# A recurrent memory transformer beside a feed-forward block: half of one weight piece is loaded into the score buffers over the step boundary

## The chip, the cores and the metric

The kernel runs on one core of a Trainium2 chip. The metric is the device time in microseconds, the median of several executions. The engines are TensorE (PE; its weight loads are listed as PEld), VectorE (DVE), ScalarE (ACT), GpSimd (POOL) and SyncE (SP); SP issues most of the transfers, which 16 DMA engines carry out.

## The reference

Two blocks on the same input of 2048 tokens by 1024 values are mixed by a gate. Block A goes through the tokens in 64 segments of 32; each segment is joined by 8 memory rows, which are the output of the segment before:

```
mem = mem0
for s in range(64):
    h = concatenate([mem, x[32*s : 32*s + 32]])           # 40 rows x 1024
    q, k, v = h @ Wq, h @ Wk, h @ Wv                      # 32 heads of 128
    p = softmax(masked(q k^T * 128**-0.5))                # per head, 40 x 40
    o = (p v) @ Wo                                        # 40 x 1024
    mem, out[s] = o[:8], o[8:]
b = (gelu(x @ w_gate) * (x @ w_up)) @ w_down
g = sigmoid((x * gate_w).sum(-1))
result = g * a + (1 - g) * b
```

All inputs are bfloat16. Each of Wq, Wk, Wv and Wo is 8 MB. Segment s needs the memory that segment s-1 gave, so the 64 steps of block A run one after the other; each uses all 32 MB of weights.

## The kernel before, in words

**Pieces and slots.** Each of the four matrices is cut into 16 pieces of 128 partitions x 2048 values (512 KB): (m, u, i) is matrix m, half u of the heads, rows i of eight. Not all 64 pieces fit on the chip. `PAIRS` (line 295) names for each matrix the i whose two pieces (u = 0 and u = 1) share one slot: three of k, three of q, four of v, four of o. These 14 slots are loaded anew in each step; all other pieces stay.

**The order.** `ORDER` (line 301) and `walk` give 64 positions per step: k0, q0, v0, k1, q1, o0, v1, o1, eight pieces each. The first round of a matrix begins with its paired pieces, the second ends with them, and `at_step` swaps u in odd steps, so the piece that a slot holds at the end of a step is the one that the next step begins with. Each slot is therefore loaded once a step: `proj` (line 653) issues a piece's products on PE and calls `spent` (358), which calls `fetch` (344), and SP issues the DMA of the slot's other piece as soon as the first has been read (line 351 in the trace, tile name sl). The first k piece of a step is (k, u, 1).

**A step.** hT holds 32 columns: 24 tokens of the segment and 8 memory rows. For each eight positions PE accumulates 128x512 products in a PSUM bank (line 662), ACT copies the bank to tok (`evac`, 568), PE transposes tok and DVE copies the result into kT or qT (`trans`, 575). The other eight rows of k, q and v of the segment (the "rest") do not depend on the memory. They are made in advance, for four segments at once, by `fill` (683) from hR; `fill_evac` (697) copies a fill's bank to a staging tile, `fill_put` (706) transposes it, copies it again and POOL stores it to qk_scr (line 719), while v goes straight to v_scr in four POOL stores (line 702). Later `load_qk` (440) and `load_v` (445) bring a segment's share back into qkr and vB, and POOL's `put_rest` (722) copies qkr into kT and qT. `scores` (594) multiplies, and DVE and ACT make the softmax in buffers laid over kT (pA, pB) and qT (tA, tB, E8). `attend` (625) multiplies with vA and vB; ACT and DVE copy into oT, POOL copies columns of oT into oRc (646). After o1 (line 674, bank XO) ACT copies the bank to a_bf, PE transposes it (840), and DVE copies the memory columns into hT (843): with that copy a step ends. POOL stores a_bf to a_scr (835).

**Staging.** a_bf lies over oT. `stage` (287) lets kT, qT, oT or tok hold a fill's copy. kT, qT and oT are 1,280 bytes per partition each and lie one behind the other.

**Fills by step.** `two` (line 735) is true in steps with s%4 of 3 or 0: there a q fill (8 pieces) and a k fill are made; in the others a v fill. Called two-fill and one-fill steps below. A k fill runs around positions q1,5 to q1,7; of the other fill three pieces run before v1 in two-fill steps, three (or five) before `attend` at o1,0, and the rest behind it. Its copies to kT and qT and its store come at o1,1 and o1,5. The last steps (from 59 on) have no fills.

**Queues.** Each engine works through its instructions in program order, with waits on semaphores that the program derives from overlapping bytes. On SP, at o1,0, stand: the load of hT for the next step, the load of qkr, the load of vB (which waits for `attend`), the store of oRc; then the fetches of the next step. A named lane orders the DMAs on it: each waits for the one before. In step 0 all rest products of segments 0 to 3 (and some of 4 to 7) are made between the normal ones (`fill0`, 764).

After the steps, at about 1776 us, memory rows of the output are made from o_scr, and block B runs in about 700 us.

## Time and profile before

| What | Value |
|---|---|
| Device time, median of 3 runs | 2480.26 us (2474.82 to 2481.07) |
| The profiled execution | 2477.56 us |
| Its span, first to last instruction | 2475.7 us |
| Granted TensorE clock, mean | 0.966 |
| PE busy | 2112.3 us, 85% |
| DVE, ACT, POOL busy | 886.7, 599.6, 449.3 us |
| Bytes moved | 642.77 MB, mean 260 GB/s |
| From the first to the last copy into hT (62 steps) | 150.6 to 1775.9 us |

A row of an instruction group gives line, engine, operation, tiles (out<-in), shapes, count, busy time, mean ns and the idle time of its engine before it with what ended that. A window row gives its length, each engine's busy time with the number of instructions, the granted clock, the DMA engines' mean busy share and GB/s. A timeline row gives start, duration, engine, line and tiles, and in brackets the idle time before it. A busy PE is not PE at its peak: products on four column groups run side by side.

### The profile page before, as it was taken

How to read it: one execution, taken by the hardware profiler on the slowest of the kernel's cores; microseconds unless marked ns; L12 is line 12 of the kernel's file. 1: busy time of each engine (PE TensorE's matmuls, PEld its weight loads, DVE VectorE, ACT ScalarE, POOL GpSimd, SP SyncE). 2: the span in 40 equal slices, each digit the busy share in tenths (PEclk: the TensorE clock that was granted, in tenths of full speed). 3: DMA queues.
4: the chain of work that ended last, by engine and by line, in shares of the span. 5: the costliest groups of instructions: out<-in, count | busy, mean ns of one | idle time of the engine just before them, and what ended most of it. 6: DMA issues, size and time to landing. Idle time of an engine off the chain costs nothing.

```text
span 2475.7 us, 76524 instructions
## 1 busy us (share of the span) xinstructions
PE 2112.3 (85%) x34822; PEld 1056.5 (43%) x34822; DVE 886.7 (36%) x2090; ACT 599.6 (24%) x1204; POOL 449.3 (18%) x886
## 2 busy tenths in 40 slices
PE   2488888888888888888888888888779999999998
PEld 1144444444444444444444444444444444444443
DVE  3223333333333333333333333333304435263452
ACT  1122222222222222222222322222203213032130
POOL 5222222222222222222222222222100000000000
PEclk9799999999999999999999999999989999999999
DMA  9869888888789888888888888988894260703406
GB/s 360 320 217 321 287 301 320 292 309 319 277 316 322 279 319 313 293 324 294 311 301 292 316 315 292 318 310 290 320 299 147 77 212 1 260 29 122 167 1 221
DMA packets 280195, 642.77 MB, mean 260 GB/s; under 512 B 30344, under 2 KB 75912, under 8 KB 279872
## 3 DMA queue, kind: packets, MB, share of 16 engines
q1 hardware_dynamic: 254560, 600.74, 67.8%
q0 software_dynamic: 14944, 22.27, 3.6%
q10 hardware_dynamic: 10368, 14.88, 1.7%
q8 instruction: 273, 4.47, 0.7%
q14 instruction: 50, 0.41, 0.0%
HBM read 606.29 MB, written 31.39 MB: 258 GB/s over the span
## 4 chain that ended last, share of the span: by engine, by line
PE 50%; DMA 35%; DVE 7%; issue 3%; ACT 3%; POOL 1%; SPq 0%; ACTq 0%; POOLq 0%; DVEq 0%
DMA sl<-in_A_Wq_dram 14%; DMA sl<-in_A_Wo_dram 14%; PE pb L662 13%; PE pb L900 13%; PE pb L674 7%; PE pb L937 6%; PE pb L691 3%; PE pb L859 2%; DMA wd<-in_B_w_down_dram 2%; PE pb L578 2%; DMA sl<-in_A_Wk_dram 2%; ACT a_bf L561 1%; DMA xr_scr<-xr 1%; PE pb L840 1%; POOL gp L428 1%
## 5 line engine op out<-in xcount | busy, mean ns | idle before, releaser
L662 PE MATMUL pb<-sl,hT 128*32 128x512 bf16 x12288 | 810.7, 394 | 95.5 <-DMA sl<-in_A_Wq_dram 39.1
L662 PEld LDWEIGHTS pb<-sl,hT 128*32 128x32 bf16 x12288 | 327.5, 99 | 422.9 <-DMA sl<-in_A_Wq_dram 58.0
L674 PE MATMUL pb<-sl,oT 128*32 128x256 bf16 x8192 | 292.8, 282 | 49.8 <-DMA sl<-in_A_Wo_dram 36.4
L561 ACT ACTIVATE tok<-pb 128x512 bf16<-128x512 f32 x320 | 191.1, 597 | 535.2 <-PE pb L662 460.5
L674 PEld LDWEIGHTS pb<-sl,oT 128*32 128x32 bf16 x8192 | 205.9, 99 | 121.0 <-DMA sl<-in_A_Wo_dram 57.2
L691 PE MATMUL pb<-sl,hR 128*32 128x512 bf16 x3072 | 218.8, 391 | 8.1 <-DMA hR<-xr_scr 4.5
L900 PE MATMUL pb<-xT,wg 128*128 128x512 bf16 x896 | 211.8, 379 | 8.4 <-DVE GT L916 8.4
L900 PE MATMUL pb<-xT,wu 128*128 128x512 bf16 x896 | 211.7, 379 | 0.0
L937 PE MATMUL pb<-wd,GT 128*128 128x512 bf16 x896 | 196.2, 379 | 6.3 <-DMA wd<-in_B_w_down_dram 6.3
L646 POOL COPY oRc<-oT 128x128 bf16<-128x128 bf16 x128 | 96.9, 757 | 478.0 <-DVE oT L564 478.0
L564 DVE COPY kT<-pb 128x512 bf16<-128x512 bf16 x128 | 54.4, 425 | 289.2 <-PE pb L578 287.0
L564 DVE COPY qT<-pb 128x512 bf16<-128x512 bf16 x128 | 54.4, 425 | 276.8 <-PE pb L578 271.7
L908 ACT ACTIVATE s<-pb 128x512 f32<-128x512 f32 x112 | 66.8, 596 | 321.7 <-PE pb L900 302.2
L900 PEld LDWEIGHTS pb<-xT,wg 128*128 128x128 bf16 x896 | 86.9, 98 | 116.4 <-DVE GT L916 12.8
L937 PEld LDWEIGHTS pb<-wd,GT 128*128 128x128 bf16 x896 | 86.5, 98 | 115.3 <-DMA wd<-in_B_w_down_dram 13.2
L900 PEld LDWEIGHTS pb<-xT,wu 128*128 128x128 bf16 x896 | 87.7, 98 | 105.7
L909 DVE SCALAR_TENSOR_TENSOR tp<-s,pb 128x512 f32<-128x512 f32 x112 | 76.9, 687 | 133.7 <-ACT s L908 133.6
L607 DVE TENSOR_REDUCE st<-pb 128x8 f32<-128x320 f32 x128 | 62.9, 492 | 164.7 <-PE pb L602 164.7
L609 ACT ACTIVATE E<-pb 128x320 bf16<-128x320 f32 x128 | 56.0, 437 | 252.8 <-DVE pb L608 252.6
L606 POOL MEMSET pB<- 128x144 f32 x128 | 27.7, 216 | 491.2 <-ACT vA L561 246.5
L561 ACT ACTIVATE vA<-pb 128x512 bf16<-128x512 f32 x128 | 76.4, 597 | 155.4 <-PE pb L662 128.0
L578 PE MATMUL pb<-ident,tok 128*128 128x128 bf16 x1024 | 103.6, 225 | 11.3 <-ACT tok L561 10.2
(81 smaller groups left out, 1775.8 us busy)
## 6 DMA issues: line engine op xcount, KB each, us to landing
sl<-in_A_Wv_dram SPq DMA_DIRECT2D x268, 512.0 KB, 11.0
sl<-in_A_Wo_dram SPq DMA_DIRECT2D x268, 512.0 KB, 7.3
sl<-in_A_Wk_dram SPq DMA_DIRECT2D x205, 512.0 KB, 5.8
sl<-in_A_Wq_dram SPq DMA_DIRECT2D x205, 512.0 KB, 8.9
wd<-in_B_w_down_dram SPq DMA_DIRECT2D x56, 1024.0 KB, 6.4
wg<-in_B_w_gate_dram SPq DMA_DIRECT2D x3, 1792.0 KB, 15.6
wu<-in_B_w_up_dram SPq DMA_DIRECT2D x3, 1792.0 KB, 13.5
qkr<-qk_scr POOLq DMA_DIRECT2D x65, 64.0 KB, 6.2
```

The source lines that it names most:

```text
L561: op("act", lambda e: e.activation(o, i, ACTF.Copy), rd=rd, wr=wr)
L564: op("dve", lambda e: e.tensor_copy(o, i), rd=rd, wr=wr)
L578: ins = e.transpose(PBV[TT][:, j * 128:(j + 1) * 128], tok[:, j * 128:(j + 1) * 128], ident[:, :])
L607: op("dve", lambda e: e.tensor_reduce(nm, sS, AX.X, ALU.max, negate=True), rd=[BK(SS)], wr=[st8.r(0, 8)])
L646: op("pool", lambda e: e.tensor_copy(oRc[:, :, 16 * u:16 * u + 16].rearrange("p c x -> p x c"), oT[:, :, :, 32:40].rearrange("p g j c -> p ...
L662: ins = e.matmul(PB[bk][32 * g:32 * g + 32, :], lhsT=h[:, i, :], rhs=w[:, g * 512:(g + 1) * 512], start=(p % 8 == 0), stop=(p % 8 == 7))
L674: ins = e.matmul(PB[XO][32 * g:32 * g + 32, 0:256], lhsT=oT[:, gp_, 2 * jj + hh, 0:32], rhs=w[:, c:c + 256], start=(r == 0 and p % 8 == 0 ...
L691: ins = e.matmul(PB[b][32 * g:32 * g + 32, :], lhsT=h[:, k[2], :], rhs=w[:, g * 512:(g + 1) * 512], start=(n == 0), stop=(n == 7))
L900: ins = e.matmul(PB[bk][:, 0:FB], lhsT=w[:, kc, cc:cc + 128], rhs=xT[:, :, :, kc, :].rearrange("p t i c -> p (t i) c"), start=(kc == 0), s ...
L908: op("act", lambda e, hg=hg: e.activation(s1[:, :], hg, ACTF.Square, scale=SQ), rd=[BK(bg)], wr=[s1.r()])
L909: op("dve", lambda e, hg=hg, t=t: e.scalar_tensor_tensor(out=t[:, :], in0=s1[:, :], scalar=1.0, in1=hg, op0=ALU.add, op1=ALU.mult), rd=[BK ...
L937: ins = e.matmul(PB[bank[2 * k + hf]][:, :], lhsT=GT[:, j, tb * 128:(tb + 1) * 128], rhs=w[:, jj, hf * 512:(hf + 1) * 512], start=(j == 0) ...
```

## The change

wP is a new tile of 128 x 1024 over kT and the first 768 bytes of qT. Over the step boundary, once `attend` of the second half has read tA and tB, SP loads into wP the first half (256 KB) of the next step's first k piece (`fetch_park`), and, behind the other loads of the boundary, the first half of that slot's other piece into the slot itself (`fetch_hi`). Behind the use of the first k piece `fetch` loads only the second half of the other piece. The products of the first position read wP and the second half of the slot. So the slot's two pieces cause three transfers of 256 KB a step instead of one of 512 KB, two of them at the boundary.

To leave kT and qT free there, fills no longer stage in them: tok is the staging tile of k and q fills, oT's place that of v fills, and a_bf moves to the tail of qT. Two-fill steps now make k and v, one-fill steps q. The v fill runs four pieces before `attend`, two at o1,6 and two behind the step's last product, while ACT copies a_bf; its copy and its four stores follow the boundary, and the two PSUM banks of the projections change places for the next step. The q fill runs wholly before `attend`; its transposes follow at o1,1. The transposes of the k fill come right behind the scores, ahead of the softmax. `put_rest` of kT moves from the third to the fourth position, `put_rest` of qT and the load of the second qkr from the third to the sixteenth. On SP, qkr's load now stands behind `fetch_park`. In step 0 all k and q rest products stage in tok, and one more v fill takes the place of one q fill. memT and hR1 move to other bytes.

```diff
-        a_bf = al("a_bf", [128, 256], at=oT.off)
-        stage = {n: al(n + "S", [128, 512], at=t.off) for n, t in (("k", kT), ("q", qT), ("o", oT))}
+        a_bf = al("a_bf", [128, 256], at=qT.off + 768)
+        wP = al("wP", [128, 1024], at=kT.off)
+        stage = {"o": al("oS", [128, 512], at=oT.off), "t": tok}
...
+        IP = PAIRS["k"][0]
+        NP_ = home["k", 0, IP]
+        def src_h(k, hf):
+            m, u, i = k
+            W = {"q": A_Wq, "k": A_Wk, "v": A_Wv}[m]
+            return W[i * 128:(i + 1) * 128, 16 * u + 8 * hf:16 * u + 8 * hf + 8, :].rearrange("d h e -> d (h e)")
+        def fetch_hi(k):
+            t = slots[NP_]
+            op("sp", lambda e: e.dma_start(t[:, 0:1024], src_h(k, 0)), wr=[t.r(0, 1024)], lane="hi")
+        def fetch_park(k):
+            op("sp", lambda e: e.dma_start(wP[:, :], src_h(k, 0)), wr=[wP.r()], lane="wP")
+        def tile(k, g, parked):
+            if parked and home[k] == NP_ and g < 2:
+                return wP[:, g * 512:(g + 1) * 512]
+            return slots[home[k]][:, g * 512:(g + 1) * 512]
...
         def fetch(n):
             k, t = uses[n][done[n]], slots[n]
+            if n == NP_:
+                op("sp", lambda e: e.dma_start(t[:, 1024:2048], src_h(k, 1)), wr=[t.r(1024, 2048)], lane=f"sl{n}")
+                return
...
         def scores():
...
+        def softmax():
             op("pool", lambda e: e.memset(pB[:, :].bitcast(FP32), 0.0), wr=[pB.r()])
...
-            f1 = fill("q" if two else "v", ub, X) if G < NG else []
-            f2 = fill("k", ub, Y) if two and G < NG else []
+            fk = fill("k", ub, Y) if two else []
+            fv = fill("v", ub, X) if two else []
+            fq = fill("q", ub, X) if one else []
...
-            def start_step():
-                if s > 0:
-                    rest(0)
-                    load_qk(s, 1)
...
-                    on("k", 0, 0, lambda: fill0("k", 0, B1, "o", 1, hR1))
-                on("q", 0, 0, lambda: fill0("q", 0, B1, "q"))
+                    on("k", 0, 0, lambda: fill0("k", 0, B1, "t", 1, hR1))
+                on("q", 0, 0, lambda: fill0("q", 0, B1, "t"))
...
+                on("v", 0, 0, lambda: fill0("v", 0, B2, "o"))
                 if NG > 1:
-                    on("q", 0, 0, lambda: fill0("q", 0, B2, "o", 1, hR1))
+                    on("v", 0, 0, lambda: fill0("v", 0, B0, "t", 1, hR1))
+            else:
+                on("k", 0, 3, lambda: put_rest(kT, 1))
+                on("q", 0, 7, lambda: (put_rest(qT, 0), load_qk(s, 1)))
...
             on("v", 1, 0, lambda: scores())
+            if two:
+                on("v", 1, 0, lambda: fill_put("k", ub, G, "t", "t", "act"))
+            on("v", 1, 0, softmax)
+            on("v", 1, 0, some(fq, 5))
             on("o", 1, 0, lambda: load_h(s + 1) if not last else None)
             on("o", 1, 0, lambda: evac(bko["v", 1], vA, "act"))
+            on("o", 1, 0, some(fq, 3))
+            if one:
+                on("o", 1, 0, lambda: fill_evac("q", ub, G, bx, "t"))
+            on("o", 1, 0, some(fv, 4))
             on("o", 1, 0, lambda: attend(ub))
+            if one:
+                on("o", 1, 1, lambda: fill_put("q", ub, G, "t", "t", "dve"))
...
+            def ahead():
+                fetch_park(at_step(0, s + 1))
+                load_qk(s + 1, 0, "sp")
+                load_v(s + 1, eng="sp")
+                o_store()
+                fetch_hi(("k", 1 - (s + 1) % 2, IP))
...
+                on("o", 1, 0, ahead)
+            on("o", 1, 6, some(fv, 2))
             for p in range(64):
                 run(at.get(p, []))
                 proj(p, s)
             act_copy(a_bf[:, :], PB[XO][:, 0:256], [BK(XO)], [a_bf.r()])
+            run(fv)
...
+            if two:
+                fill_evac("v", ub, G, bx, "o")
+                X, Y = Y, X
```

## The prediction

> **What bounds the kernel now.** I read the page first (shares, the chain that ended last, the DMA issues), then the start of every step (the copy into hT at L843), then one step in windows, then the instructions around a step boundary.
>
> ```profile
> DMA  9869888888789888888888888988894260703406
> PE 50%; DMA 35%; DVE 7%; issue 3%; ACT 3%; POOL 1%; SPq 0%; ACTq 0%; POOLq 0%; DVEq 0%
> DMA sl<-in_A_Wq_dram 14%; DMA sl<-in_A_Wo_dram 14%; PE pb L662 13%; PE pb L900 13%; PE pb L674 7%; PE pb L937 6%; PE pb L691 3%; PE pb L859 2%; DMA wd<-in_B_w_down_dram 2%; PE pb L578 2%; DMA sl<-in_A_Wk_dram 2%; ACT a_bf L561 1%; DMA xr_scr<-xr 1%; PE pb L840 1%; POOL gp L428 1%
> ...
> sl<-in_A_Wv_dram SPq DMA_DIRECT2D x268, 512.0 KB, 11.0
> sl<-in_A_Wo_dram SPq DMA_DIRECT2D x268, 512.0 KB, 7.3
> sl<-in_A_Wk_dram SPq DMA_DIRECT2D x205, 512.0 KB, 5.8
> sl<-in_A_Wq_dram SPq DMA_DIRECT2D x205, 512.0 KB, 8.9
> ```
>
> DMA is 80 to 90% busy through the whole recurrent stage, the chain spends 30% of the span on weight pieces, and a 512 KB piece takes 5.8 to 11 us to land: they queue behind each other. The copy into hT closes a step:
>
> ```profile
> L843 DVE COPY hT<-pb x63: 190/192/192, 150.6 to 1775.9; 128x64 bf16<-128x64 bf16 x63
> ```
>
> 62 steps in 1625.3 us, 26.21 us each. Step 34 (1017.97 to 1043.40) in windows; behind PE, PEld, DVE, ACT and POOL stand the granted clock, the DMA share and GB/s:
>
> ```profile
> 1018.00:1020.00 2.00, 1.99 (x40) 1.01 (x44) 0.00 (x0) 0.03 (x1) 1.05 (x2) 1.00 0.47 70
> 1020.00:1022.00 2.00, 2.00 (x40) 0.93 (x36) 0.42 (x1) 0.57 (x1) 1.17 (x3) 1.00 0.89 279
> 1022.00:1026.00 4.00, 4.00 (x101) 1.93 (x93) 1.42 (x3) 1.21 (x3) 0.21 (x1) 1.00 1.04 356
> ...
> 1038.00:1040.00 2.00, 1.97 (x76) 1.56 (x76) 0.56 (x2) 1.10 (x3) 0.77 (x1) 1.00 1.04 375
> 1040.00:1042.00 2.00, 0.87 (x32) 0.31 (x22) 0.00 (x0) 0.00 (x0) 1.92 (x4) 1.00 0.72 214
> 1042.00:1044.00 2.00, 1.23 (x18) 0.51 (x22) 0.19 (x1) 0.38 (x1) 1.16 (x3) 0.85 0.22 46
> ```
>
> DMA is full from about 2 us into the step until 22 us and nearly empty around the boundary. The end of that step, in the timeline:
>
> ```profile
> 1040.64 0.40 PE L674 MATMUL pb<-sl,oT 128*32 128x256 bf16 x8 [0.19 <-DMA sl<-in_A_Wo_dram]
> 1041.98 0.40 PE L674 MATMUL pb<-sl,oT 128*32 128x256 bf16 x8 [0.94 <-DMA sl<-in_A_Wo_dram]
> 1042.43 0.38 ACT L561 ACTIVATE a_bf<-pb 128x256 bf16<-128x256 f32 x1 [2.64 <-PE pb L674]
> 1042.87 0.29 PE L840 MATMUL pb<-ident,a_bf 128*128 128x128 bf16 x2 [0.49 <-ACT a_bf L561]
> 1043.20 0.19 DVE L843 COPY hT<-pb 128x64 bf16<-128x64 bf16 x1 [4.19 <-PE pb L840]
> 1043.44 1.05 PE L662 MATMUL pb<-sl,hT 128*32 128x512 bf16 x8 [0.28 <-DVE hT L843]
> 1044.11 0.33 SPq L351 DMA_DIRECT2D sl<-in_A_Wk_dram  x1
> ```
>
> The last two Wo pieces arrive one by one; 0.5 us after the last one a_bf is copied, 1.0 us later the step ends, and 0.5 to 0.7 us into the next step its first fetch goes out. From the trace's issue and landing times, averaged over 62 steps and counted from the step's start, the pieces land at: Wk 4.9, 6.8, 8.7; Wq 10.6, 12.0, 13.5; Wv 14.9, 16.2, 17.5, 18.8; Wo 20.3, 21.7, 23.2, 24.6; then hT 24.9, qkr 25.2, vB 25.5, o_scr 25.7. The last Wo is issued near 16, so it stands in a queue that never runs dry. In one-fill steps (s%4 is 1 or 2) a_bf follows Wo by 0.5 us in almost every step; in two-fill steps on average by 0.8. So the loop is: first fetch, 14 pieces in line, last Wo, boundary. Between 1.5 us before the boundary and 1.2 us after it 2.0 to 2.3 us of DMA time (all 16 engines) lie unused.
>
> **The change, part by part.**
>
> *Half a piece leaves the full stretch.* Of the first k piece only 256 KB are fetched behind its use; 13.5 pieces stand before the last Wo. Price of half a piece: successive Wv pieces (4,096-byte rows) land 1.31 us apart, so half is 0.65; with 2,048-byte rows (Wo, 1.43 apart) the remaining half costs 0.72, the saving then is 0.60. Upper end: successive Wk pieces land 1.9 us apart, half is 0.95 to 1.0. I take 0.65, because the Wk distance holds other work (qkr, a_scr) that stays. 63 steps (1 to 63): 41 us, ends 38 and 63.
>
> *The two halves at the boundary.* Both copies go out on SP behind attend (end at 20.5 in one-fill, 21.6 in two-fill steps), so behind Wo in line: hT, issued at 19.4 to 20.8, lands 0.25 us after Wo. The parked half then lands 0.25 + 0.72 = 0.97 us after Wo; its first reader starts 1.5 us after Wo. Cover 0.5 us, cost 0. Without cover (a 128 KB store from POOL in between, 0.46 us of packet time) up to 0.3 a step, 19 us. The other half follows qkr, vB and o_scr: about 2.4 us after Wo, 0.9 into the next step, when the first new fetch barely starts. Both take 1.45 us of the 2.0 to 2.3 unused. Cost 0; traffic grows by 0.26 MB a step.
>
> *SP's order.* qkr no longer goes out before attend ends: issued some 1.5 us later and 0.7 further back, it lands at about the boundary. Its user, the POOL copy into kT, moves to the fourth piece (0.65 us in). vB is used after 10 us. Cost 0.
>
> *POOL.* The qT copy and the second qkr load move from the third to the sixteenth piece. The qT copy now waits for the store of a_bf, which lies in qT's tail: issued near -0.5, landing 4 to 5 us later, so near 4; DVE's write of qT comes at 5.0. qkr then is issued near 4.5 and lands 6.1 later (its row today), before 11; its reader is the fortieth piece, past 12. In exchange vA no longer waits for that store (21.0 us in 9 steps today, mostly covered). Cost 0; a late store costs at most 0.5 in some steps.
>
> *v fill over the boundary, in 31 steps.* Four v_scr issues of 0.556 us stand behind a_scr: POOL is free near 2.5, the kT copy ends at 2.9, DVE needs it at 3.3. Their 128 KB fall into the full stretch; today the q store (128 KB) goes out around the boundary. 4,096-byte packets on that queue take 229 ns, 32 of them on 16 engines 0.46 us; today's q store already delays the first Wk by 0.2 (5.0 against 4.8). I take 0.2 more, 6 us, ends 0 and 14. The vA copy (6.2) has to wait for these stores to read oS: last issue near 2, landing by 4.5 to 7; the Exp behind it is due at 7.9, so nothing.
>
> *Products.* Two v pieces (0.43 us) run while ACT copies a_bf, in a PE gap of 0.49. In two-fill steps the q transposes (0.33) leave the stretch after attend; the k copy on ACT comes before Exp (0.6 us against DVE's 1.0). In one-fill steps three fills (0.65) move ahead of attend, into a wait for tB of 0.85 to 0.95, and transposes (0.33) come behind it. All this frees PE where Wo binds: gain 0, ends -10 and 0. The one-fill q store goes out nearer the Wo tail than today's v stores: 0.1 in 32 steps, 3 us, ends 0 and 10.
>
> *Clock.* In one-fill steps PE waits 0.3 to 0.6 longer for Wo. The windows show half clock for 3.41 us at a time, in most cases, 30 times from step 1 to 63, after stretches of equal length with only 0.9 to 2.6 us of idle; the 52 first products of a step then take 4.63 us instead of 2.99, and the step's mean is 0.4 to 0.6 longer. Eight more such steps: 4 us, ends 0 and 10. The Trainium skill (TensorE: Matmul & The Clock Gate, Part 1) has the clock fall after a window of about 3.4 us that is idle; by that rule this term would be 0. The rows above show falls after far less idle, so the trace does not agree.
>
> *Step 0.* Its k and q results are now staged in tok alone. Today the q_k stores land 5.6, 6.4, 6.8 and 5.5 us after issue and each waits for the one before; now the copy out of PSUM, the transposes and the second copy (1.8 us) join that wait, one store leaves it and a second set of v stores enters. Following the chain I get the first attend near 119.5 instead of 115.9, and 2 us more at the last fill: 6 us, ends 0 and 12.
>
> Sum: -41 + 6 + 3 + 4 + 6 = -22. The profiled execution took 2477.56 us (span 2475.7), 2.7 below the median of the three runs, 2480.26, and inside their spread. 2477.6 - 22 = 2456.
>
> **Rivals.**
>
> *A. Another limit takes over in two-fill steps.* There a_bf follows Wo by 0.8 on average, so in part of them PE, not Wo, ends the step. If only the 32 one-fill steps gain, and the v fill costs half: -21 + 16 = -5, 2472. Against it: attend could end at 20.6 in two-fill steps (softmax behind the earliest scores at 15.9), and 2.2 us of products behind it end before the new Wo landing (24).
>
> *B. The half pieces are slow; slower than before.* They read 2,048 bytes out of every 8,192; no transfer today does that (Wo's rows are contiguous). Wo's own packets take 88 ns in the stream, but 207 at its start. A half has 8 packets on each of 16 engines. With c for its time in the full stretch the steps gain 63 x (1.31 - c) against the 19 us of small costs: nothing is left at c = 1.01 us (126 ns a packet), 0.3% is lost from 1.13 (141 ns), and at 1.66 (207 ns) the parked half also lands 0.4 us too late: 22 + 26 + 19 = 67, 2545. For it: nothing measured. Against: whole pieces, 4,096 of 8,192, run at 162 ns, the full rate. The Trainium skill (DMA: Bandwidth & Descriptors, Latency and other measured facts) reports rates falling to half for row pitches of large powers of two, from 512 KiB up; whether 8 KiB suffers no run here shows.
>
> *C. The half piece is worth what Wk's distance says*, 0.95, with the small costs at half: -60 + 9, 2427.
>
> *D. The unused time at the boundary cannot be used,* so 0.26 MB more is 0.7 us more a step: 2520. That would be the change not doing what it says. Against it: hT, qkr, vB and o_scr already run there at 0.2 to 0.3 us apiece.
>
> **Chances.** Forecast (2442 to 2466) 0.52; A 0.17; C 0.13; B 0.14; D 0.04. A measurement can tell about 0.3%, 7.4 us: faster is below 2472.8. Faster: 0.52 + 0.13 + half of A = 0.74; same: the rest of A and the mild end of B, 0.11; slower: 0.15. The range 2428 to 2488 leaves out some 0.06 below and 0.13 above.
>
> **What the new profile would show.** Right: steps of about 25.6 us; last Wo landing near 24.0 with a_bf 0.5 behind; DMA share up by about 3 points, the boundary windows near 0.7; hardly any PE wait for the parked tile at the first piece; step 0 ending near 157. Wrong: PE waiting for wP at each boundary, half-piece packets well over 100 ns (B); a_bf more than 0.8 behind Wo with unchanged steps (A); the first Wk landing later than 5 us (D); ACT waiting for tok's stores at the ninth piece.

## The result, and the profile after

The changed kernel takes 2488.49 us (median of 15 runs, 2476.99 to 2497.87), the kernel before beside it 2477.89 us (2469.57 to 2487.76). The ratio is 1.0042, with a 95% interval of 1.0022 to 1.0061: slower by 0.4%, where 2456 and faster was forecast. The profiled execution took 2488.98 us, with a span of 2487.1 us. Of all executions in this document one ran in a slower state of the chip (a_vearly_3, 2510 us); it is left out of that run's median and ratio.

The page of the changed kernel, in the same order as before (DMA share in 40 slices, the chain that ended last by engine and by line, the DMA issues with their median time to landing):

```profile
DMA  9859989899899998899899998999994160613506
PE 47%; DMA 36%; DVE 8%; issue 3%; ACT 3%; POOL 2%; SPq 0%; ACTq 0%; POOLq 0%
DMA sl<-in_A_Wo_dram 13%; PE pb L942 13%; DMA sl<-in_A_Wq_dram 13%; PE pb L696 10%; PE pb L708 7%; PE pb L979 6%; DMA v_scr<-oS 4%; PE pb L722 3%; PE pb L901 2%; PE pb L610 2%; DMA wd<-in_B_w_down_dram 2%; DMA qk_scr<-tok 1%; DVE st L645 1%; DVE pA L647 1%; ACT E L643 1%
...
sl<-in_A_Wv_dram SPq DMA_DIRECT2D x268, 512.0 KB, 10.9
sl<-in_A_Wo_dram SPq DMA_DIRECT2D x268, 512.0 KB, 7.2
...
sl<-in_A_Wk_dram SPq DMA_DIRECT2D x140, 512.0 KB, 6.5
...
sl<-in_A_Wk_dram SPq DMA_DIRECT2D x129, 256.0 KB, 3.8
wP<-in_A_Wk_dram SPq DMA_DIRECT2D x64, 256.0 KB, 4.1
```

The DMA engines are busier, as forecast: the packets of the queue that carries the weights took 70.9% of their time, 67.8% before. The weights' part of the chain went down a little (Wo 14% to 13%, Wq 14% to 13%). New in the chain stands a store: `v_scr<-oS`, 4%. The tile's own view of the copy into hT, and who waited for the parked tile:

```profile
L882 DVE COPY hT<-pb x63: 190/192/193, 159.1 to 1790.6; 128x64 bf16<-128x64 bf16 x63
...
DMA wP<-in_A_Wk_dram: 3.2, 5
```

Step 0 ends at 159.1 us instead of 150.6, the 62 steps behind it take 1631.5 us instead of 1625.3. PE waited for the parked half in 5 steps only, 3.2 us in all. So the parked half comes in time; the gain that it should have brought is missing elsewhere. By kind of step, means of the profiled executions in us over steps 1 to 58, which hold all the fills (the later steps have none):

| s%4 | before | after | what surrounds it |
|---|---|---|---|
| 3 | 26.51 | 26.45 | first two-fill step |
| 0 | 26.56 | 27.43 | two-fill, right behind a v fill |
| 1 | 25.91 | 25.84 | one-fill, right behind a v fill |
| 2 | 26.09 | 25.94 | one-fill |

Only one kind became longer, by 0.87 us. Step 44 (1294.87 to 1322.54, one of that kind) shows how. ACT, POOL and SP in the timeline, each line with start, duration, engine, line, tiles and the idle time before it:

```profile
1294.35 0.60 ACT L593 ACTIVATE oS<-pb 128x512 bf16<-128x512 f32 x1
...
1295.33 2.19 POOL L733 DMA_DIRECT2D v_scr<-oS  x4
...
1303.77 0.60 ACT L593 ACTIVATE vA<-pb 128x512 bf16<-128x512 f32 x1 [4.11 <-DMA v_scr<-oS]
...
1310.29 1.64 SPq L379 DMA_DIRECT2D sl<-in_A_Wo_dram  x2
```

The v fill's bank is copied to oS, whose bytes vA needs; POOL issues the four stores until 1297.5; vA may be written at 1303.77, 8.9 us into the step. In before the same copy starts at 6.4 in most steps of this kind. Behind vA come E, the softmax, the first `attend`, the first o products, and with them the first Wo fetch: 15.4 us into the step. As medians over the steps with s%4 of 0: first `attend` 11.6 (before 10.55), first Wo fetch issued 15.3 (14.4), last Wo landed 25.4 (24.75). Windows of step 44 around that issue show what this makes of the DMA engines (length, busy time of PE, PEld, DVE, ACT and POOL with instructions, granted clock, DMA share, GB/s):

```profile
1309.87:1310.87 1.00, 1.00 (x37) 0.78 (x30) 0.00 (x0) 0.60 (x1) 0.00 (x0) 1.00 0.97 377
1310.87:1311.87 1.00, 1.00 (x36) 0.88 (x36) 0.42 (x1) 0.60 (x1) 0.00 (x0) 1.00 0.68 150
1311.87:1312.87 1.00, 0.87 (x44) 0.39 (x33) 0.00 (x0) 0.00 (x0) 0.00 (x0) 1.00 0.99 348
1312.87:1313.87 1.00, 0.97 (x21) 0.61 (x24) 0.69 (x2) 0.40 (x1) 0.00 (x0) 1.00 0.91 270
```

In the second of them, before Wo's packets come, a third of the DMA time lies unused. The waits of ACT in after give the sum:

```profile
ACT vA L593 <- PE pb L696: 143.2, 103, 3.5
...
ACT vA L593 <- DMA v_scr<-oS: 86.0, 24, 4.9
```

### The profile page after: what moved, and what is told of

It is laid out like the page before. It is cut to its first block, busy times and chain, and to the rows that moved or that the text cites. A ratio compares the mean times of both kernels' runs of the same rounds, so it can differ in the third digit from the quotient of the medians.

```text
span 2487.1 us, 76750 instructions
## 1 busy us (share of the span) xinstructions
PE 2097.9 (84%) x34796; PEld 1065.9 (43%) x34822; DVE 884.9 (36%) x2085; ACT 597.3 (24%) x1209; POOL 448.1 (18%) x886
## 3 DMA queue, kind: packets, MB, share of 16 engines
q1 hardware_dynamic: 272992, 617.26, 70.9%
## 4 chain that ended last, share of the span: by engine, by line
PE 47%; DMA 36%; DVE 8%; issue 3%; ACT 3%; POOL 2%; SPq 0%; ACTq 0%; POOLq 0%
DMA sl<-in_A_Wo_dram 13%; PE pb L942 13%; DMA sl<-in_A_Wq_dram 13%; PE pb L696 10%; PE pb L708 7%; PE pb L979 6%; DMA v_scr<-oS 4%; PE pb L722 3%; PE pb L901 2%; PE pb L610 2%; DMA wd<-in_B_w_down_dram 2%; DMA qk_scr<-tok 1%; DVE st L645 1%; DVE pA L647 1%; ACT E L643 1%
## 5 line engine op out<-in xcount | busy, mean ns | idle before, releaser
L696 PE MATMUL pb<-sl,hT 128*32 128x512 bf16 x12160 | 785.3, 386 | 60.4 <-DMA sl<-in_A_Wq_dram 28.9
L696 PEld LDWEIGHTS pb<-sl,hT 128*32 128x32 bf16 x12160 | 321.0, 97 | 365.5 <-DMA sl<-in_A_Wq_dram 44.2
L708 PE MATMUL pb<-sl,oT 128*32 128x256 bf16 x8192 | 299.4, 284 | 72.2 <-DMA sl<-in_A_Wo_dram 33.9
L593 ACT ACTIVATE tok<-pb 128x512 bf16<-128x512 f32 (+1 forms) x356 | 212.6, 597 | 525.5 <-PE pb L696 403.5
L722 PE MATMUL pb<-sl,hR 128*32 128x512 bf16 x3068 | 225.9, 395 | 14.3 <-DMA hR<-xr_scr 7.9
L722 PEld LDWEIGHTS pb<-sl,hR 128*32 128x32 bf16 x3068 | 84.5, 99 | 73.0 <-issue 25.4
L610 PEld LDWEIGHTS pb<-ident,tok 128*128 128x128 bf16 x1024 | 59.4, 99 | 108.8 <-ACT tok L593 81.7
```

Of the source, the lines that this page charges most:

```text
L593: op("act", lambda e: e.activation(o, i, ACTF.Copy), rd=rd, wr=wr)
L610: ins = e.transpose(PBV[TT][:, j * 128:(j + 1) * 128], tok[:, j * 128:(j + 1) * 128], ident[:, :])
L696: ins = e.matmul(PB[bk][32 * g:32 * g + 32, :], lhsT=h[:, i, :], rhs=tile(k, g, walk[p][1] == 0), start=(p % 8 == 0), stop=(p % 8 == 7))
L708: ins = e.matmul(PB[XO][32 * g:32 * g + 32, 0:256], lhsT=oT[:, gp_, 2 * jj + hh, 0:32], rhs=w[:, c:c + 256], start=(r == 0 and p % 8 == 0 ...
L722: ins = e.matmul(PB[b][32 * g:32 * g + 32, :], lhsT=h[:, k[2], :], rhs=tile(k, g, parked), start=(n == 0), stop=(n == 7))
```

## The experiments

All times are medians against the kernel before on the same chip (2476 to 2479 us). A short diff stands for each edit; "-" are lines of the kernel that it is made from, "+" the new ones, and "..." stands for code left out. Several of these kernels use stale weights or rows in order to leave a transfer out, as their expectations say: they are there for the time alone. The intervals reach 5 to 7 us to each side (9 to 12 for b_reload, a_mended_whole, b_no_k1 and b_half_v_nofill), so two runs less than some 8 us apart are not told apart.

| Run | us | Ratio to before [95%] |
|---|---|---|
| b_half | 2462.1 | 0.9939 [0.9914, 0.9964] |
| b_reload | 2509.6 | 1.0129 [1.0081, 1.0177] |
| b_reload2 | 2487.3 | 1.0044 [1.0021, 1.0067] |
| a_whole | 2495.5 | 1.0075 [1.0053, 1.0096] |
| a_step0 | 2474.9 | 0.9998 [0.9971, 1.0025] |
| a_vstatic | 2481.1 | 1.0021 [0.9993, 1.0049] |
| a_vact | 2494.3 | 1.0065 [1.0036, 1.0093] |
| a_vearly | 2468.9 | 0.9971 [0.9950, 0.9992] |
| a_vearly_3 | 2474.7 | 0.9994 [0.9972, 1.0016] |
| a_mended | 2506.6 | 1.0109 [1.0084, 1.0134] |
| a_mended_whole | 2510.1 | 1.0123 [1.0075, 1.0172] |
| b_nofill | 2464.4 | 0.9935 [0.9911, 0.9960] |
| b_half_nofill | 2448.3 | 0.9875 [0.9850, 0.9901] |
| b_half_rows | 2464.2 | 0.9958 [0.9939, 0.9978] |
| b_half_v | 2459.5 | 0.9928 [0.9907, 0.9950] |
| b_half_k3 | 2459.2 | 0.9935 [0.9910, 0.9961] |
| b_no_k1 | 2443.4 | 0.9876 [0.9832, 0.9919] |
| b_half_v_nofill | 2447.9 | 0.9891 [0.9854, 0.9929] |

### The parts of the change, one by one

**b_half**: the kernel before, half a k piece less in the stretch and nothing else.

```diff
+            if n == home["k", 0, 1] and done[n] > 0:
+                op("sp", lambda e: e.dma_start(t[:, 1024:2048], A_Wk[..., 16 * u + 8:16 * u + 16, :]...), wr=[t.r(1024, 2048)], lane=lane)
+                return
```

> The kernel before, but behind its use the first k slot gets only the second half of its other piece; the first half is never loaded again, so a part of the weights is stale. It has the saving of the change without its price: no transfers at the boundary, no rearranged tail. Theory 1 (a half piece is worth what the clean steps of the changed kernel show, 0.35 to 0.55 us a step): 62 to 63 steps, 22 to 35 us, so 2443 to 2456 against a before near 2478. Rival (the stretch isn't what sets the step; the half piece buys nothing): above 2470. Second rival (the 0.65 us of my prediction was right and the changed kernel loses it elsewhere): 2430 to 2440.

Measured: 15.7 us less (interval 9 to 21), 0.25 us in each of 63 steps. The term that I had put at 0.65 a step is the first that failed.

**b_reload and b_reload2**: the kernel before with two more transfers of 256 KB at the boundary, over data that are there already. In the first, one of them was ordered by a read of tA, which made later writers of tA wait; the second orders both behind `attend` alone.

```diff
+                    op("sp", lambda e: e.dma_start(t[:, 0:1024], W[i * 128:(i + 1) * 128, 16 * u:16 * u + 8, :]...),
-                       rd=[tA.r()] if p == 0 else [], wr=[t.r(0, 1024)], lane=lane)
+                       wr=[t.r(0, 1024)], lane=lane, after=[att[0]])
```

> The kernel before, with the two boundary transfers of the change added and nothing saved: behind attend SP loads the first half of the next k piece once more over itself, and behind the o_scr store half of a v piece over itself (needed again only at the seventeenth position). Two more 256 KB transfers with 2,048-byte rows a step. Theory 1 (they run in DMA time that lay unused): at most 0.15 us a step, 2478 to 2487. Rival (they push the next step's first fetches back or hold up the first product): 0.3 to 0.7 us a step, 2497 to 2520.

> The kernel before with two more boundary transfers, as in the earlier run, but ordered behind attend's products alone: that run also made later writers of qT wait for the transfer, which put 0.55 us between a_bf and hT in the two-fill steps. Theory (the transfers themselves are nearly free): 0.05 to 0.2 us a step, 2481 to 2491. Rival (they cost what the earlier run showed, by pushing the next fetches back): 2503 or more.

Measured: b_reload 32 us more, which is mostly the order I had added: in its two-fill steps the step ended 1.7 us behind the start of the copy to a_bf, and 0.95 in the others and in before. b_reload2 says what the transfers cost: 9 us more, 0.14 a step, for which I had said 0. The first whole k piece lands at 4.9 to 5.3 us instead of 4.7 to 4.8.

**a_whole**: the changed kernel without parking, the k piece fetched whole as before.

```diff
-            if parked and home[k] == NP_ and g < 2:
+            if False:
...
-                fetch_park(at_step(0, s + 1))
...
-                fetch_hi(("k", 1 - (s + 1) % 2, IP))
```

> The changed kernel with its whole rearranged tail and staging, but the first k piece is loaded whole as before: no parked half, no boundary transfers. Theory 1 (the rearranged staging costs some 25 to 35 us, of which 8.5 in step 0 and the rest from the v stores behind the boundary, and the parked half earns 15 to 30 of it back): 2500 to 2515. Rival (the rearrangement is neutral, and the boundary transfers cost what the half piece earns or more): 2478 to 2490.

Measured: the rearrangement alone costs 17.7 us. Parking is worth 7.0 us on top of it (2495.5 to 2488.5), which agrees with b_half and b_reload2 together: -15.7 + 8.6 = -7.1.

**a_step0**: the changed kernel with step 0 staged as before, and parking from step 1 on.

```diff
-                fill_evac(m, r, G, b, st)
-                fill_put(m, r, G, "t", "t", "act")
+                fill_evac(m, r, G, b, "t" if m != "v" else st)
+                fill_put(m, r, G, "t", st)
```

> The changed kernel, but step 0 stages its results as before (in kT, qT and oT), loads the first k piece whole, and parks from step 1 on. Theory (step 0 lost 8.5 us to one staging tile that waits for its own stores): the first copy into hT back from 159 to at most 151 us, the whole 8 to 12 us below the changed kernel, 2477 to 2481. Rival (the time of step 0 is hidden or comes back later): within 3 us of the changed kernel.

Measured: 13.6 us less than after, even with before. The first copy into hT starts at 140.2 us, against 159.1 in after; the steps behind it are no shorter (1632.7 us).

### The stores of v behind the boundary

**a_vstatic**: the late v stores read a tile of weights that nothing writes, so vA waits for no store. **a_vact**: the stores are issued by ACT instead of POOL.

```diff
-                        st[32 * g:32 * g + 32, :].rearrange(...)), rd=[st.r()], ...
+                        (stv if late else st)[32 * g:32 * g + 32, 0:512].rearrange(...)), rd=[(stv if late else st).r()], ...
...
-                    op("pool", lambda e, g=g: e.dma_start(
+                    op("act" if late else "pool", lambda e, g=g: e.dma_start(
```

> The changed kernel, but the v stores behind the boundary (31 steps) read a weight slot that never changes in place of oS, so vA has nothing to wait for in them; same stores, same bytes, same queue; the stored v rows are wrong. Theory 1 (the wait of ACT's vA copy for these stores, with Exp behind it, delays attend and with it the o fetches in the two-fill steps that follow): 0.7 to 1.0 us in the 15 steps with s%4 of 0 and up to 0.2 in those with 1, so 10 to 18 us below the changed kernel, 2471 to 2479. Rival (the stores cost by their traffic in the full stretch, not by the wait): within 4 us of the changed kernel.

> The changed kernel with the v stores behind the boundary issued by ACT instead of POOL, right behind ACT's copy into oS; all else equal, the result is right. Theory (vA waits for these stores in 24 of 31 steps, till 6.7 to 9.7 us into the step; ACT's queue issues them 0.5 us apart less and they land earlier): 4 to 9 us below the changed kernel, 2479 to 2485, and the vA waits for v_scr gone or under half. Rival (the full stretch makes any store land that late, whichever queue issues it): within 3 us.

Measured: without the wait 7.4 us less than after, with intervals that just overlap. The trace bears the wait out: vA is copied at 6.4 us again in 11 of 14 steps with s%4 of 0, and these steps take 26.78 us in place of 27.43. From ACT's queue nothing is gained (2494.3). **a_vearly** goes one further: the same number of stores, of the static tile, issued at the piece o1,1, before the boundary.

```diff
+            if two:
+                on("o", 1, 1, lambda: v_store(ub, G, slots[home["k", 0, 0]]))
...
-                fill_evac("v", ub, G, bx, "o")
+                fill_evac("v", ub, G, bx, "o", True)
```

> The changed kernel, but the 31 sets of v stores are issued before the boundary, at o1,1, and read a weight slot that never changes (the stored v rows are wrong). Compared with the run in which they read that slot at their place behind the boundary, only the place of 128 KB of traffic differs. Theory (behind the boundary it falls into the full stretch and costs 0.2 to 0.4 us): 5 to 12 us below that run (2481), 2469 to 2476. Rival (its place is worth nothing, or it now holds up the last Wo): 2478 or more.

Measured: 19.6 us less than after; set against a_vstatic, 12 of them come from the place of the 128 KB. In the steps behind a v fill the last Wq piece lands at 13.1 us into the step instead of 13.7 in a_vstatic (medians). POOL's four issues move as well, but do not show as a cause: its copy into kT starts at 0.5 instead of 2.6 us, and DVE's next write of kT stands at 3.4 in both. The late v stores cost some 20 us together. **a_vearly_3** moves only those whose boundary leads into another two-fill step.

```diff
-            if two:
+            if two and s % 4 == 3:
...
-                fill_evac("v", ub, G, bx, "o", True)
+                fill_evac("v", ub, G, bx, "o", s % 4 == 3)
```

> a_vearly with the stores of v moved ahead of the boundary only in the steps with s%4 of 3, whose boundary leads into another two-fill step (there they store values of a weight slot instead of the fill's, so that part of v is wrong); the steps with s%4 of 0 keep their stores behind the boundary. After measured 2488 and a_vearly 2469. Theory C: the late stores cost where a two-fill step follows, because there vA, the first attend, the four Wo fetches and PE behind them move together (mean step of s%4 of 0: 27.4 us in after, 26.3 in a_vearly; of s%4 of 1: 25.8 and 25.5): three quarters of the 20 us come back, 2473. Theory D: each late store costs the same, 10 of 20 come back: 2478.

Measured: 13.8 of the 19.6 us come back, between what the two theories gave, and its interval (2470 to 2480) holds both. The means by kind of step speak for theory C: s%4 of 0 falls to 26.31 us, as in a_vearly (26.33), and s%4 of 1 stays at 25.78 (after 25.84, a_vearly 25.49).

**a_mended and a_mended_whole** try to make that real: a_step0 with the whole v fill before the boundary, staged in tok, with parking and without.

```diff
+            if two:
+                on("o", 1, 4, lambda: fill_evac("v", ub, G, bx, "t"))
...
-            run(fv)
-            if two:
-                fill_evac("v", ub, G, bx, "o")
-                X, Y = Y, X
```

> The changed kernel with both losses mended, the result right: step 0 staged as before (parking from step 1 on), and in two-fill steps the whole v fill runs before the boundary (four pieces before attend, two each at o1,1 and o1,3), is copied to tok at o1,4 and stored from there; the k fill's transposes move ahead of the scores (o0,7), so that tok is free in time. Theory (step 0 is worth 10 to 13 us, the v stores' wait and place 12 to 20): 2456 to 2468, below the kernel before by 0.4 to 0.9%. Rival (tok, shared by two stores, now holds up ACT at the end of the step or at the ninth piece, and gives it back): 2470 or more.

> The mended kernel without the parked half: the first k piece is loaded whole, no transfers at the boundary. What differs from the mended kernel is the parked half alone. Theory (a half piece less is worth 0.25 us a step, its two boundary transfers cost 0.15): 3 to 9 us above the mended kernel. Rival (the parked half is worth nothing, the gain is the tail's): within 3 us of it.

Measured: 31.7 us more than a_step0. The waits of ACT and of PE at tok in a_mended:

```profile
ACT tok L590 <- DMA v_scr<-tok: 136.5, 26, 6.9
...
L607 PE MATMUL pb<-ident,tok 128*128 128x128 bf16 x1024 | 104.7, 226 | 63.7 <-ACT tok L590 60.6
```

tok is written again at the ninth piece of each step, some 2 us behind the boundary, and has to wait for the v stores that read it; the first `attend` slips to 12.5 us in steps with s%4 of 0 and to 13.3 with 1. By the trace, then, the wait only changed its tile; no run takes that wait out of a_mended. Parking is worth 3.5 us there, within the intervals.

### Why half a piece is worth 0.25 us and not 0.65

**b_nofill and b_half_nofill** take the fills of segments 8 to 63 away, first with the whole k piece, then with the half: if PE's fills end the steps, the half should be worth more without them.

```diff
-            f1 = fill("q" if two else "v", ub, X) if G < NG else []
-            f2 = fill("k", ub, Y) if two and G < NG else []
+            f1 = fill("q" if two else "v", ub, X) if G < 2 else []
+            f2 = fill("k", ub, Y) if two and G < 2 else []
```

> The kernel before without the fills of segments 8 to 63 (their products, copies, transposes and stores are left out; the later steps read the rest rows of segments 0 to 7). Only to be set against the next run. With one-third less for PE to do beside the pieces I expect steps of 24.5 to 25.5 us, 2420 to 2440.

> The same without those fills, and with only half of the first k slot reloaded, as in the earlier run of the kernel before (there it gained 16 us with the fills in place). Theory (without fills nothing but the pieces' arrival ends a step, so the half piece is worth its full landing gain, 0.4 to 0.65 us a step): 25 to 41 us below the run without fills. Rival (a half piece at the head of the line is worth 0.25 us whatever PE has to do): 12 to 20 us below it.

Measured: leaving all the fills out gains 13 to 14 us, where I had expected 40 or more, and the half is worth 16.0 us without them, as with them. That does not clear the fills, since the clock changed too. Without them the granted clock was 0.94, with them 0.97: of steps 1 to 58, 41 in b_nofill and 44 in b_half_nofill hold more than 0.5 us at half clock, 28 in before. In the steps at full clock alone the fills are worth some 0.7 us (means of 26.12 in before and 25.36 in b_nofill), and the half without them 0.2 (25.15), with an error of 0.13. The DMA share in the first stretch of a step fell too: of the stretch from 2 to 8 us 0.21 us lay unused in b_nofill and 0.60 in b_half_nofill, means over 62 steps. That gave three theories, on place, packets and another end, and four runs.

**b_half_rows**: half the rows of the first k piece, so half the packets. **b_half_v**, **b_half_k3**: half of the fourth v piece, of the third k piece. **b_no_k1**: no reload of the first k slot at all.

```diff
+            if n == home["k", 0, 1] and done[n] > 0:
+                op("sp", lambda e: e.dma_start(t[64:128, :], src(k)[64:128]), wr=[t.r()], lane=lane)
+                return
...
+            if n == home["v", 0, 6] and done[n] > 0:
+                op("sp", lambda e: e.dma_start(t[:, 1024:2048], A_Wv[..., 16 * u + 8:16 * u + 16, :]...), wr=[t.r(1024, 2048)], lane=lane)
+                return
```

> The kernel before, in which the slot of the first k piece is reloaded after step 0 with 64 of its 128 rows only (256 KB in 4,096-byte rows; the other rows keep the piece of step 0, so part of the k products uses old weights). In b_half the same bytes left, but the number of packets stayed, and the step gained 0.25 us. Theory P (place): the first transfer of a step runs while the DMA engines are not yet full (without fills their share at 2 to 5 us into the step was 0.95, 0.97, 0.99 with the whole piece, 0.75, 0.88, 0.95 with the half), so half of what leaves there is only idle time: about 2462 again. Theory S (packets): the start of the stretch is paid by the packet, the half has as many as the whole; with half of them the 0.65 us come back: 2437. Theory E (another end): PE's own chain ends the step, and no transfer is worth more than 16 us in all: 2462.

> The kernel before, in which the slot of the fourth paired v piece is reloaded after step 0 with its second half only (256 KB in 2,048-byte rows; part of the v products uses old weights). This transfer lies in the middle of the stretch, where the share is 1.0. Theory P: 0.65 us in 63 steps, 41 us: 2437. Theory S: 2,048-byte packets in the stream took 88 ns, so the half costs 0.70 instead of 1.31 and 38 us are gained: 2440. Theory E: 2462.

> As b_half, but for the third paired k piece instead of the first (part of the k products uses old weights). It runs at 7 to 8.7 us into the step, where the share is already 0.97 to 1.0. Theory P: nearly all of 0.65 us a step, 2437 to 2445. Theory S: k rows are read with as many packets, 2462. Theory E: 2462.

> The kernel before without any reload of the slot of the first k piece after step 0 (512 KB a step less; the k products of odd steps use the other half's weights). Theory P: the idle start stays where it is and is met by the next piece: 0.25 + 0.65 us a step, 57 us, 2421. Theory S: the whole 1.31 us, 82 us, 2396. Theory E: no more than 16 to 20, 2460.

Measured: 12, 17, 17 and 33 us less. All three theories fall as they stood. Not the packets (rows: 12). Not the place alone (v and k3 in the full stretch: no more than the first piece). And no fixed end either: twice the bytes give twice the gain. Each 256 KB is worth about 0.26 us a step (0.20 by b_half_rows, each uncertain by 0.1), 40% of the 0.65 that its transfer takes, at every place that was tried.

The landing times say where the rest goes. Medians over the steps, in us from the step's start; the last two columns are the DMA time not used in two stretches of a step, means of 62 steps:

| Run | first k | last v | first Wo issued | first Wo | last Wo | unused 2 to 8 | unused 15 to 20 |
|---|---|---|---|---|---|---|---|
| before | 4.80 | 18.66 | 14.18 | 20.18 | 24.50 | 0.26 | 0.07 |
| b_half | 4.30 | 18.38 | 14.06 | 19.82 | 24.09 | 0.47 | 0.16 |
| b_half_k3 | 4.79 | 18.19 | 14.06 | 19.62 | 23.92 | 0.32 | 0.23 |
| b_half_v | 4.85 | 17.98 | 14.20 | 19.57 | 24.09 | 0.23 | 0.32 |
| b_nofill | 5.10 | 18.46 | 14.02 | 19.96 | 24.18 | 0.21 | 0.09 |
| b_half_nofill | 4.23 | 18.46 | 14.01 | 19.80 | 24.08 | 0.60 | 0.08 |
| b_half_v_nofill | 5.11 | 17.86 | 14.02 | 19.50 | 23.87 | 0.21 | 0.29 |

Without its half the last v piece lands 0.68 us earlier in b_half_v, the whole price. But the next transfer, Wo, is issued at the same 14.2 us. Its first fetch goes out when PE has read the slot in the first o product. That product stands in program order behind the first `attend`, behind the last q products, which need the step's Wq pieces, and in two-fill steps behind the k fill. Step 34 of before (one-fill) shows what PE waits for there, with `attend` done at 1028.8:

```profile
1031.14 0.40 PE L662 MATMUL pb<-sl,hT 128*32 128x512 bf16 x4 [0.88 <-DMA sl<-in_A_Wq_dram]
1031.37 1.05 PE L674 MATMUL pb<-sl,oT 128*32 128x256 bf16 x32
...
1031.80 1.92 SPq L351 DMA_DIRECT2D sl<-in_A_Wo_dram  x4
```

Between `attend` and the first o product PE waits for Wq 1.1 us per one-fill step of before, and 0.1 per two-fill step, where the k fill's products keep it busy. So in one-fill steps the issue of Wo hangs on the same queue, and in two-fill steps on PE. The half v piece stands in line behind Wq and can move neither. In before Wo's first packets run at about 16 us, 2 us after the issue, and the last v packets end at 17 to 18 (medians): the queue is ahead by roughly 1 us. Half a piece takes 0.65 of that, and where a step asks for Wo late, nothing is left. In b_half_v 23 of 62 steps have more than 0.3 us unused between 15 and 20 us, in before 4. Step 8 (two-fill) of b_half_v from 14 to 18 us, where Wo was issued at 346.07, 14.8 into the step:

```profile
345.31:346.31 1.00, 0.91 (x32) 0.79 (x36) 0.00 (x0) 0.45 (x1) 0.04 (x1) 1.00 1.00 399
346.31:347.31 1.00, 1.00 (x36) 0.68 (x28) 0.26 (x1) 0.41 (x2) 0.00 (x0) 1.00 0.79 293
347.31:348.31 1.00, 1.00 (x51) 0.64 (x42) 0.16 (x1) 0.33 (x1) 0.00 (x0) 1.00 0.72 260
348.31:349.31 1.00, 1.00 (x52) 0.68 (x44) 0.62 (x2) 0.00 (x0) 0.22 (x1) 1.00 1.02 379
```

The same stretch of step 8 of before, with Wo issued at 348.85, 14.1 into the step, is full:

```profile
348.80:349.80 1.00, 1.00 (x34) 0.68 (x28) 0.00 (x0) 0.44 (x1) 0.00 (x0) 1.00 1.03 418
...
350.80:351.80 1.00, 1.00 (x45) 0.63 (x49) 0.36 (x1) 0.00 (x0) 0.22 (x1) 1.00 1.06 393
```

**b_half_v_nofill** asks whether the two-fill steps make that limit (in b_half_v the one-fill steps were 0.5 us shorter, the two-fill steps 0.3 longer).

```diff
+            if n == home["v", 0, 6] and done[n] > 0:   # as in b_half_v, on b_nofill
```

> b_half_v and b_nofill together: the kernel before without the fills of segments 8 to 63 (their shares are read from older segments) and with only the second half of the fourth paired v piece reloaded. b_nofill measured 2464. Theory A (the two-fill steps are bound by PE behind the second attend, the one-fill steps by Wo): without fills all steps are of the second kind and gain 0.5 us, as the one-fill steps of b_half_v did: 62 x 0.5 = 31, 2433. Theory W (Wo's four fetches are issued behind the first attend, at 14.0 us, whatever left the queue before; the queue then runs dry ahead of them, 0.23 us in b_half_v): a part of it stays idle with fills or without, 0.25 us a step, 2449. Theory P as it stood (0.65 everywhere in the middle of the stretch): 2424.

Measured: 16.5 us less than b_nofill, the number of theory W (2449; 2447.9 measured) and not that of A. W's reason holds in part: 0.20 us more lie unused ahead of Wo, and the step gains 0.26. But Wo is issued at 14.0 because Wq lands 0.7 us ahead of it (median), and not because of `attend`: PE still waits for Wq, 0.8 to 0.95 us a step. As in b_nofill the clock is low (0.945; 39 of steps 1 to 58 hold half clock), so this run does not clear the two-fill steps either.

What the trace shows, then: of 0.65 us 0.2 to 0.4 turn into unused DMA time, for the first k piece in the first stretch of the step, for the others mostly ahead of Wo; the last Wo lands 0.3 to 0.6 earlier (0.1 in b_half_nofill); and a further 0.1 to 0.3 is lost between the last Wo and the copy into hT, above all in two-fill steps.

The same traces, sorted by kind of step and clock, tell more. Means over those of steps 1 to 58 that run at full clock, in us from the step's start (in brackets the number of steps):

| Run | one-fill: Wo issued | last Wo | step | two-fill: Wo issued | last Wo | step |
|---|---|---|---|---|---|---|
| before | 14.01 | 24.27 | 25.72 (10) | 14.49 | 24.55 | 26.32 (20) |
| b_half | 13.67 | 23.97 | 25.42 (19) | 14.29 | 24.15 | 26.19 (23) |
| b_half_rows | 13.98 | 24.12 | 25.57 (20) | 14.24 | 24.14 | 25.96 (18) |
| b_half_k3 | 13.74 | 23.87 | 25.32 (16) | 14.32 | 23.97 | 25.91 (19) |
| b_half_v | 14.04 | 23.88 | 25.34 (20) | 14.52 | 24.41 | 26.28 (20) |
| b_no_k1 | 13.01 | 23.13 | 24.68 (21) | 14.25 | 24.03 | 25.99 (21) |

In the one-fill steps the queue sets everything: in each of the ten steps of before Wo is issued 0.71 us after the last Wq lands, and the step ends 1.45 us after the last Wo. There the whole k piece is worth 1.04 of its 1.31 us, and half a piece 0.15 to 0.4. In the two-fill steps PE, busy with the k fill, holds Wo's issue near 14.25, and the whole piece brings 0.33. A mean of a step is uncertain by 0.1 to 0.2 us, and these are single executions, sorted afterwards; no run changes the two-fill steps at an unchanged clock. Why places so different come to the same 0.26 over all steps stays open.

## Why the prediction was wrong

The terms as the prediction had them, and what the runs gave:

| Term | Forecast | Measured |
|---|---|---|
| half a piece leaves the stretch | -41 (38 to 63) | -16 (b_half), -16 (without fills) |
| two halves at the boundary | 0, up to 19 | +9 (b_reload2) |
| v fill over the boundary | +6 (0 to 14) | about +20 (a_vearly), 7 of them vA's wait |
| step 0 | +6 (0 to 12) | +8.5 in the trace, +13.6 by a_step0 |
| products, SP's order, POOL, q store, clock | +7 | about -11, the remainder |

With the trace's 8.5 for step 0 the measured terms make +21.5, the kernel is 10.6 slower; the remainder of -11 is a difference of medians, not a run. Step 0's 8.5 is the low end: the eleven traces with the old step 0 reach the first copy into hT at 145.5 to 150.6 us, the six with the new one at 158.1 to 161.3, some 11 us apart in the middle. The v fill ran in 29 steps, not 31.

**The half piece.** The step that failed first is "Half a piece leaves the full stretch", priced at the distance between landings: 41 us, and 15.7 came. The sentence beside it, that the last Wo "stands in a queue that never runs dry", is true of the kernel before, and the byte count itself makes it so: its first Wo fetch, issued at 14.2, lands at 20.2, while the last v lands at 18.7. I took a busy share of 1.0 for a bound, without asking what would idle once less stood in line. "So the loop is: first fetch, 14 pieces in line, last Wo, boundary" leaves out that Wo is issued in the middle of the step, behind the landing of Wq in one-fill steps and behind PE's k fill in two-fill steps. No end of my range for this term (38 to 63) was as low as 16. Where the rest of the 0.65 goes is shown in part only: 0.2 us and more into idle DMA time, and the two-fill steps gain less by the traces.

**The v fill.** This is the other step that failed, 6 us forecast and about 20 measured. The working had the stores' landing right (4.5 to 7; they landed 5.3 us after issue in the median, 7.6 at most) and drew the wrong line from it: "the Exp behind it is due at 7.9, so nothing". The Exp waits for vA on ACT, and in the steps with s%4 of 0 vA came at 7.9 to 9.7 in 11 of 14 steps. What stood behind it I had not followed: E, softmax, `attend`, the first o product, the Wo fetches, PE's end of a two-fill step. The 128 KB in the full stretch cost 12 us beside that, 0.4 us a step, where I took 0.2, 6 in all.

**The boundary copies.** The cover of 0.5 us held: PE waited 3.2 us for wP in all. The price by b_reload2 was the other one, the next step's first k piece, later by 0.1 to 0.5 us. "Which barely starts" was no reason for 0.

**Step 0.** The direction and its cause were right, the size (6) was near the trace's 8.5; a_step0 gained more, since its first copy into hT comes 10 us ahead of before's as well. **Products.** The remainder hints that the rearranged products gain more than my "0, ends -10 and 0"; no run takes them alone. **Clock.** I took eight half-clock stretches more; between the first and the last copy into hT the records show 21 of 3.41 us each instead of 31.

**The rivals.** B ended on the right side, and its 1.01 us for a half, at which nothing is left, is close to 1.31 - 0.25 = 1.06. But its mechanism, slow rows of 2,048 bytes, is not the reason: in the stream they took 84 ns in the median (b_half_v), not the 126 that B needs, and b_half_rows, with 4,096-byte rows and half the packets, gains no more. A named PE in the two-fill steps, and the means of b_half_v and b_no_k1 by kind of step look like it (one-fill steps 0.5 and 1.1 us shorter, two-fill steps between 0.3 shorter and 0.3 longer). With the fills gone the gain stays 16 us, but under a lower clock, so A is neither shown nor ruled out. It is not the whole loss, since one-fill steps at full clock gain less than 0.65 from half a piece too. D (the unused time cannot be used, 2520) was too dark: 9 us. C falls.

Of the signs named, a_bf 0.5 behind Wo (in the median), a DMA share 3 points up and hardly any wait for wP came. Steps of 25.6 us (26.3), the last Wo near 24.0 (24.3 in the median), boundary windows near 0.7 (0.54, from 0.20 before) and step 0 at 157 (159.1) did not.

## What to carry to other kernels

A queue that is full tells what its transfers cost now, not what leaving one out is worth: look for the next transfer that is issued late, what its issue waits for (a computation, or a landing in the same queue), and how much other work the queue holds until then. In this kernel the answer differed from one kind of step to the next. A store that reads a buffer over a loop's boundary has to land before that buffer's next writer, and everything behind that writer belongs to its price, up to the fetches that the late work would have issued. Leaving work out can change the clock too, as the runs without fills show; compare the granted clock before reading their difference. Test the cheap half of a change alone: leaving the half piece out in the old kernel told in one run that 41 us were never there. No version here beat both kernels beyond the measurement; a_step0, the nearest with the full computation, is even with before.

## What the runs showed of the hardware

PE's "issue" gaps (idle time in which it waited for nothing that the profile shows) make 24 us in before and 27 in after over the 62 steps. Those over 0.4 us each end 1.2 to 1.6 us after a 16 KB packet of the queue that the profile calls instruction ends (274 packets in after, about 1.0 us each, beside a full queue of weights). An example from step 44 of after, where such a packet ran from 1317.92 to 1318.90:

```profile
1320.15 0.60 PE L722 MATMUL pb<-sl,hR 128*32 128x512 bf16 x5 [0.89 <-issue]
```

Without fills these gaps fall to 11 us, in b_half_v they are 32. That PE had run out of instructions there was not tested.

Around the boundary the time to landing did not follow the size: 256 KB took 3.8 us (the slot's halves) and 4.1 (wP) in the median, the whole first k piece, 512 KB, 4.3 in before. The stores of v, 32 KB each, took 5.3 in the median, 2.1 at the least and 7.6 at most, and issuing them from ACT's queue instead of POOL's brought no gain.

Half clock came without a long idle stretch. In the kernel before there are 29 half-clock stretches between the first and the last copy into hT; in the 3.41 us ahead of each, PE was idle for 1.5 to 2.6 us. In b_nofill there are 58.
